# A gated mix of two attention branches: channel order of branch B's output, one ratio tile, merged write-outs, the gate turned by TensorE, and a new instruction order

## Chip, cores and metric

The kernel runs on one core of a Trainium2 chip. The metric is the device time of one execution in microseconds (us). All five engines are used: PE (TensorE, matmuls), ACT (ScalarE), DVE (VectorE), POOL (GpSimd) and SP (SyncE, which here issues nearly all DMAs). Each engine works through its own instructions strictly in order; semaphores tie them together.

## What is computed

`x` is 2048 tokens by 640 channels, 32 heads of 20 channels. Branch A is a linear attention with softmax features, branch B a segment-wise causal attention with a compressive memory; a gate per token mixes them.

```python
x = A_x
g = sigmoid((x * gate_w).sum(-1, keepdims=True))
# branch A: phi(k) = [softmax(k w_phi), softmax(-k w_phi)], same for q
o_A = (phi_q @ (phi_k^T v)) / (phi_q @ sum(phi_k) + 1e-6)
# branch B: 4 segments of 512 tokens, per head
p     = softmax(q k^T * scale + causal mask);  a_dot = p @ v
a_mem = (pq @ M) / (pq @ z + 1e-6)      # M, z: sums over earlier segments
o_B   = sigmoid(beta) * a_mem + (1 - sigmoid(beta)) * a_dot
out = g * (o_A @ A_wo) + (1 - g) * (o_B @ B_wo)
```

## The kernel before

**Order.** The program builds a graph of operations and then emits them in an order that stands in it as a table (`ORDER`, one base-36 number per operation). Two more tables say on which engine an operation with a choice runs (`CHOICE`: an evacuation of PSUM on ACT or DVE, the scaling of `E` on DVE or POOL) and which buffer each tile takes (`WHERE`). Nothing is decided at run time: each engine's queue is a fixed list, waits are derived from the data and buffer dependences.

**Stages.** Early in the span the projections of branch B for segment 0, its attention, and the keys and values of branch A (`a_k`, L887 on, and the sums over tokens `acc`, L956, and `KVZacc`) run side by side; the last `acc` addition ends at 166 us. After it come the queries of branch A, segment by segment (`a_q`: `ET` L1015, ratio round trip `zb`, `zc`, `rx`, `rr`, products L1047, matmuls L1062, `oA` L1071), beside the remaining attention of branch B, and the output matmuls (`final`, L1090/1091) per 128-token tile.

**Branch B's attention** (`b_step`, once for each of 4 segments and 8 groups of 4 heads, spread over the span up to 309 us): QK matmuls (L763), exponentials on ACT (L772), causal masks on POOL (L776), PV matmuls (L804). The PV output sits in PSUM as 4 blocks of 32 partitions, one block per head: rows 0 to 19 are the channels, row 20 the softmax denominator, already divided by 1 - sigmoid(beta) through a column of `v1B`. It is copied to `oU` (`evac`, L608 on ACT or L609 on DVE). `oU` holds two groups.

**Leaving `oU`** (end of `b_step`): per pair of groups, SP issues four DMAs that write the denominators to the DRAM tensor `dn` and four that write the channels to `opk`, one each per block of 32 partitions. With 4 segments and 4 pairs that is 64 and 64.

**The ratio** (`b_out`, once per segment): `dc` is read back from `dn` as 128 x 128 (32 KB), `rqB` is its reciprocal (L835), and L836 multiplies it by `og`, one minus the gate, which arrives in the same layout through DRAM (`gt`, one write and four reads per segment, end of `b_proj`, L476). The product is written to DRAM 20 times, once for each channel of a head (`rxB<-dc`, 4 DMAs of 160 KB), and read back as `rrB`, 128 x 5 x 512 (640 KB). `oP`, 128 x 5 x 512, holds the channels in their natural order (row p of chunk c is channel 128 c + p), so each chunk needs a ratio of its own. L844 multiplies `oP` by `rrB`, L884 adds `moT`, the memory part: for each of the 4 token tiles of a segment, matmuls L866/867, a reciprocal (L875), one DVE product from PSUM into `mo` (L876, 128 x 640) and a DMA transpose into `moT` (L473). Then `final` multiplies `oTA` and `oP` by `Wo`, whose second half is `B_wo` in the same natural order (`load_wo`).

Output tiles, `oA` and `mo` share a pool of four buffers of 1280 bytes; output tiles may take two more inside the projection weights `WB` once these are done.

Of the kernel before, what the change touches and what calls it, by code (L numbers as in the profile page):

```python
# [70 lines left out]
002211073310534000222133101014230232135210305133220
# [1108 lines left out]
```

## Time and profile before

| | us |
|---|---|
| median of 3 runs (lowest, highest) | 368.99 (367.27, 371.01) |
| the profiled execution's own time | 370.18 |
| its span, first to last instruction | 368.4 |
| busy: PE / ACT / DVE / POOL | 290.6 / 252.0 / 227.7 / 120.7 |

The mean granted TensorE clock is 0.907 of full speed. The profile's chain, followed back from the last instruction, divides the span as PE 29%, DVE 25%, DMA 22%, ACT 10%, SP's queue 9%, issue 4%. Durations and waits are those of the one profiled execution; a wait is put down to what released it last. The rows that the prediction uses stand in a section of their own below.

### The profile page before, as it was taken

The numbers are of one execution on the slowest core, as the hardware profiler recorded it, in microseconds if no ns is written. First come the engines' busy times: TensorE is split into PE (matmuls) and PEld (weight loads), VectorE is DVE, ScalarE is ACT, GpSimd is POOL, SyncE is SP. The second block draws the span as 40 slices with busy tenths as digits, with TensorE's granted clock in tenths as the row PEclk, the third lists the DMA queues.
The fourth block names the chain that finished last, engine by engine and source line by source line (L and its number), as shares of the span: only waits on it lengthen the run. The fifth ranks groups of instructions, "written<-read, shape, count | busy, mean of one in ns | idle before, by whom it ended". The sixth has DMA issues, their size and how long they took to land.

```text
span 368.4 us, 7093 instructions
## 1 busy us (share of the span) xinstructions
PE 290.6 (79%) x2811; PEld 151.1 (41%) x2852; DVE 227.7 (62%) x370; ACT 252.0 (68%) x332; POOL 120.7 (33%) x136
## 2 busy tenths in 40 slices
PE   2999899988799999699639957897997666093686
PEld 2355445544444544263324523344443323052343
DVE  1544679998999999997527832638534631443440
ACT  4377899897699999589726964888799996010011
POOL 2022653656356155642501101432434553000000
PEclk9999999999999999899868996999999955579669
DMA  7987550302424310142356996883555636735851
GB/s 216 259 168 167 93 122 1 52 2 45 74 50 69 79 33 8 14 127 75 118 145 170 155 44 153 227 158 55 121 144 158 60 85 167 182 98 128 207 146 56
DMA packets 88880, 40.80 MB, mean 111 GB/s; under 512 B 68080, under 2 KB 86416, under 8 KB 88848
## 3 DMA queue, kind: packets, MB, share of 16 engines
q1 hardware_dynamic: 88096, 39.50, 50.1%
q10 hardware_dynamic: 656, 0.82, 0.6%
q8 instruction: 22, 0.36, 0.4%
q0 software_dynamic: 96, 0.04, 0.3%
q14 instruction: 10, 0.08, 0.1%
HBM read 16.37 MB, written 13.16 MB: 80 GB/s over the span
## 4 chain that ended last, share of the span: by engine, by line
PE 29%; DVE 25%; DMA 22%; ACT 10%; SPq 9%; issue 4%; POOL 1%; DVEq 0%; ACTq 0%
PE ps L629 7%; SPq L477 7%; DVE acc L956 6%; PE ps L1090 6%; ACT expT L772 5%; DMA oTA<-oA 4%; DVE z L914 3%; DMA moT<-mo 3%; PE ps L901 3%; DMA zb<-zs 2%; PE ps L763 2%; PE ps L651 2%; DMA kT<-qkm 2%; DMA xtok<-in_A_x_dram 2%; PE ps L1091 2%
## 5 line engine op out<-in xcount | busy, mean ns | idle before, releaser
L772 ACT ACTIVATE expT<-ps 128x1024 bf16<-128x1024 f32 x128 | 124.4, 1037 | 23.2 <-PE ps L763 22.4
L776 POOL TENSOR_SCALAR_AFFINE_SELECT expT<-expT 128x512 bf16<-128x512 bf16 x96 | 69.0, 727 | 104.5 <-ACT expT L772 95.1
L629 PE MATMUL ps<-xT,WB 128*128 128x512 bf16 x192 | 50.3, 397 | 1.5 <-DVE xT L609 0.7
L608 ACT ACTIVATE out<-ps 128x640 bf16<-128x640 f32 x7 | 4.9, 704 | 52.7 <-PE ps L1091 32.6
L763 PE MATMUL ps<-qkm 20*128 20x384 bf16 (+3 forms) x320 | 22.0, 326 | 19.7 <-DVE oU L609 7.2
L772 ACT ACTIVATE ej<-ps 128x1024 bf16<-128x1024 f32 x32 | 31.6, 1046 | 6.6 <-PE ps L763 6.6
L916 POOL TENSOR_TENSOR E<-E,z 128x1280 bf16<-128x1280 bf16 x12 | 28.8, 2404 | 20.5 <-DVE z L915 17.6
L776 POOL TENSOR_SCALAR_AFFINE_SELECT ej<-ej 128x1024 bf16<-128x1024 bf16 x16 | 18.5, 1157 | 47.8 <-ACT ej L772 42.0
L1090 PE MATMUL ps<-Wo,oTA 128*128 128x512 bf16 x77 | 27.4, 439 | 7.9 <-DVE mo L876 4.8
L956 DVE TENSOR_TENSOR acc<-acc,E 64x1280 bf16<-64x1280 bf16 x31 | 31.0, 1001 | 1.7 <-POOL E L916 1.0
L1091 PE MATMUL ps<-Wo,oTA 128*128 128x128 bf16 x80 | 19.4, 242 | 11.9 <-DVE mo L876 11.5
L804 PE MATMUL ps<-expT,v1B 128*21 128x384 bf16 (+2 forms) x384 | 24.9, 331 | 4.9 <-POOL expT L776 1.6
L629 PEld LDWEIGHTS ps<-xT,WB 128*128 128x128 bf16 x200 | 18.2, 101 | 23.2 <-issue 5.7
L1090 PE MATMUL ps<-Wo,oP 128*128 128x512 bf16 x78 | 26.5, 423 | 0.0
L914 DVE TENSOR_REDUCE z<-E 128x64 f32<-128x1280 bf16 x16 | 23.7, 1479 | 3.2 <-ACT E L908 3.1
L1015 ACT ACTIVATE ET<-ps 128x512 bf16<-128x512 f32 x40 | 22.8, 614 | 3.8 <-PE ps L1010 2.3
L901 PE MATMUL ps<-WvA,xT 128*128 128x512 bf16 x77 | 22.7, 379 | 1.9 <-ACT eg L655 1.1
L908 ACT ACTIVATE E<-ps 128x640 bf16<-128x640 f32 x32 | 22.5, 708 | 1.1 <-PE ps L902 0.6
L1010 PE MATMUL ps<-xT,WqA 128*128 128x512 bf16 x91 | 21.8, 380 | 1.8 <-issue 0.8
L609 DVE CAST out<-ps 128x640 bf16<-128x640 f32 x9 | 7.4, 823 | 25.0 <-PE ps L1091 23.2
L651 PE MATMUL ps<-WvB,xT 128*128 128x512 bf16 x72 | 22.6, 393 | 0.2 <-ACT ej L772 0.2
L901 PE MATMUL ps<-WkA,xT 128*128 128x512 bf16 x73 | 21.8, 380 | 0.0
(126 smaller groups left out, 554.7 us busy)
## 6 DMA issues: line engine op xcount, KB each, us to landing
opk<-oU SPq DMA_DIRECT2D x64, 40.0 KB
oP<-opk SPq DMA_DIRECT2D x4, 640.0 KB
rxB<-dc SPq DMA_DIRECT2D x16, 160.0 KB
rx<-rc SPq DMA_DIRECT2D x16, 160.0 KB
rr<-rx SPq DMA_DIRECT2D x4, 640.0 KB
rrB<-rxB SPq DMA_DIRECT2D x4, 640.0 KB
out_dram<-out SPq DMA_DIRECT2D x16, 160.0 KB
scr<-qkm SPq DMA_DIRECT2D x16, 120.0 KB
```

The costliest lines, as they stand in the source:

```text
L477: return e.dma_start(a, b)
L629: r = e.matmul(self.pf(pt, 0, 0, LSEG), lhsT=self.WB[:, w, kc, 128 * c:128 * (c + 1)], rhs=xT[:, kc, LSEG * n:LSEG * (n + 1)], start=(kc = ...
L651: e.matmul(self.pf(pt, 0, 0, 512), lhsT=l, rhs=self.WvB[:, kc, 0:512], start=(kc == 0), stop=(kc == 4))
L763: r = e.matmul(self.pf(pts[i // 2], i % 2, c0, N), lhsT=view(32 * i, 32 * i + DH, 1, 128 * j, 128 * (j + 1)), rhs=view(32 * i, 32 * i + DH ...
L772: self.op("act", d_act(1024), lambda e, p=p, o=o: e.activation(o(), self.pbanks(pts[p], 0, 2, 512), ACT.Exp, scale=scale), W=[(pts[p], 0), ...
L776: self.op("pool", d_pool(n_el), lambda e: e.affine_select(view(), view(), pattern=pat, compare_op=ALU.is_ge, fill=0.0, base=0, channel_mul ...
L901: e.matmul(self.pf(pt, 0, 0, 512), lhsT=l, rhs=W[:, kc, 0:512], start=(kc == 0), stop=(kc == 4))
L914: self.op("dve", 1.48, lambda e: e.tensor_reduce(z[:, :], Ev(), axis=AX.X, op=ALU.add), R=[(E, 0), (E, 1)], W=[(z, "*")], claim=[rz], pr=p ...
L916: self.op(("dve", "pool"), {"pool": d_pool(1280, 2), "dve": 1.56}, lambda e: e.tensor_tensor(Ev(), Ev(), rz[:, :].rearrange("p (h o) -> p ...
L956: self.op("dve", 0.9, lambda e, src=src: e.tensor_tensor(acc[lo:lo + 64, :], acc[lo:lo + 64, :], src(), ALU.add), R=[(self.Et[t], 0), (sel ...
L1090: e.matmul(self.pf(pt, 0, 0, 512), lhsT=l, rhs=self.Wo[:, c, 0:512], start=(c == 0), stop=(c == 9))
L1091: r = e.matmul(self.pf(pt, 1, 0, 128), lhsT=l, rhs=self.Wo[:, c, 512:640], start=(c == 0), stop=(c == 9))
```

## The change

- Branch B's output rows are dealt out so that partition 4 h + r of `oP` holds channels 5 r to 5 r + 4 of head h, one per chunk. One 128 x 512 ratio then serves all five chunks: `rxB` is written once (32 KB, one DMA instead of four of 160 KB), read back as 128 KB instead of 640 KB, and L844's product reads it broadcast over the chunks. `B_wo` is loaded in that row order, and `mo` is written in it by two DVE instructions of 128 x 320 instead of one of 128 x 640.
- `opk` holds `oU` as it is, 128 rows per group with denominators and padding: one DMA of 256 KB per pair of groups instead of eight. `dc` (rows 20 of each block) and `oP` (rows 0 to 19) are both read from it.
- The gate's way through DRAM (`gt`, `og`) is gone. Four fp32 matmuls per segment (`omg` broadcast to 32 columns against an fp32 identity) put one minus the gate into PSUM in the layout of `dc`, and the product L836 reads it there. The identity costs a memset and a POOL instruction at the start.
- Output tiles may take five buffers in `WB` instead of two. Four PE spin matmuls instead of six.
- `ORDER`, `CHOICE` and `WHERE` are new throughout.

```diff
-NSPIN = 6
+NSPIN = 4
...
-CHOICE = "001100011111110001011010100001010101011111000010111011000011111111110010101001010101111001110110100000111100001101001101111111110001100101010010011011111101000001"
+CHOICE = "100111000110011010110010101110011111101111111111101101101001001111001100101000010010101111110011110100111111001101101011001100000101010001010111111010111101011001"
...
-        for i in range(2):
-            sl = Slot(self.WB.off + 10240 + 1280 * i)
+        for i in range(5):
+            sl = Slot(self.WB.off + 5120 + 1280 * i)
...
-        gt, gtT = self.gt[n % 2]
-        og = self.sbt("og", [128, 128], FP32, self.p_og)
-        self.dma("sp", gt.rearrange("q t -> t q"), self.omg[:, sl], R=[(self.omg, n)], W=[(gtT, "*")], pr=prg + 1, noncontig=True, name="gtw", issue=0.5, lat=3.0)
-        for q in range(4):
-            self.dma("sp", lambda q=q, og=og: og[q:128:4, :], gt[q:q + 1, :].rearrange("o t -> (o t)").partition_broadcast(32), R=[(gtT, "*")], W=[(og, q)],
...
-            for i in range(4):
-                self.dma("sp", dn.rearrange("(g i o) t -> i o g t", i=4, o=1)[i][:, gs, :], lambda oU=oU, i=i: oU[32 * i + DH:32 * i + DH + 1, :, :],
...
-            for i in range(4):
-                self.dma("sp", opk.rearrange("(g i d) t -> i d g t", i=4, d=DH)[i][:, gs, :], lambda oU=oU, i=i: oU[32 * i:32 * i + DH, :, :],
...
+            self.dma("sp", opk[slice(g0, g + 1, g - g0)].rearrange("g p t -> p g t"), lambda oU=oU: oU[:, :, :],
...
-        self.dma("sp", lambda: dc[:, :], dn.rearrange("h (q t) -> (h q) t", q=4), R=[(dnT, "*")], W=[(dc, "*")], pr=pr, name="dr", issue=0.4, lat=1.8)
-        self.dma("sp", lambda: oP[:, :, :], opk.rearrange("(c p) t -> p c t", p=128), R=[(opT, "*")], W=[(oP, c) for c in (0, 3)], pr=pr, name="opr", issue=0.4, lat=4.0)
+        hv = opk.rearrange("g (i r) t -> (g i) r t", r=32)
+        self.dma("sp", lambda: dc[:, :], hv[:, DH, :].rearrange("h (q t) -> q h t", q=4), R=[(opT, "*")], W=[(dc, "*")], pr=pr, name="dr", issue=0.45, lat=1.7)
+        self.dma("sp", lambda: oP[:, :, :].rearrange("p c t -> p (c t)"), hv[:, 0:DH, :].rearrange("h (d c) t -> h d (c t)", c=NCH),
...
+        gp = self.pst("og", 1)
+        def ogm(e):
+            for q in range(4):
+                b = 512 * gp.t[0]
+                r = e.matmul(self.ps[32 * q:32 * q + 32, b:b + 128], lhsT=self.omg[:, 4 * n + q:4 * n + q + 1].to_broadcast([128, H]), rhs=self.identF[:, :],
...
-        for q in range(4):
-            self.dma("sp", rx.rearrange("h f (q t) -> q h f t", q=4)[q],
-                     lambda q=q: dc[q:128:4, :].rearrange("p (o t) -> p o t", o=1).to_broadcast([32, DH, 128]),
...
+        self.dma("sp", rx.rearrange("h (q t) -> q h t", q=4), lambda: dc[:, :], R=[(dc, "*")], W=[(rxT, "*")], pr=pr, name="rxw", issue=0.5, lat=2.0)
+        self.dma("sp", lambda: rr[:, :], rx.rearrange("h (o t) -> h o t", o=1).to_broadcast([H, 4, LSEG]), R=[(rxT, "*")], W=[(rr, "*")], pr=pr, name="rxr", issue=0.45, lat=2.2)
...
-        wB = self.ins["B_wo"].rearrange("(c p) n -> p c n", p=128)
+        wB = self.ins["B_wo"].rearrange("(p c) n -> p c n", c=NCH)
```

What each engine now has: SP issues 176 DMAs instead of 320. DVE has 396 instructions instead of 372 (among them 5 more evacuations of `qkm`, 4 more of `v1B`, 2 fewer of `vA`, 2 more of `zs`, 2 more scalings of `E`, 24 products into `mo` instead of 12), ACT 326 instead of 335.

SP's queue near the end of the program, before the change, from the write-outs of the last group pairs to the read of the last ratio (`oU_319` is the last pair, `oU_300` and `oU_308` older ones, `dc_333` and `rrB_340` the last segment's ratio):

```order
L477 DMA dn<-oU_319 2x1x512 x4
L476 DMA og_322<-gt 32x128 x2
L477 DMA opk<-oU_319 20x2x512 x2
L477 DMA opk<-oU_300 20x2x512
L477 DMA dc_333<-dn 128x128
L473 DMA_TRANSPOSE moT_323<-mo_325 128x5x128
L477 DMA opk<-oU_319 20x2x512
L477 DMA opk<-oU_308 20x2x512
L477 DMA opk<-oU_319 20x2x512
L477 DMA rxB<-dc_333 640x1x128 x4
L473 DMA_TRANSPOSE moT_323<-mo_329 128x5x128
L477 DMA oP_339<-opk 128x5x512
```

The same place after it (`oU_321` is the last pair, `oU_302` the one before, `dc_330` and `rrB_341` the last ratio):

```order
L472 DMA opk<-oU_302 128x2x512
L472 DMA rr_296<-rx 128x5x512
L468 DMA_TRANSPOSE oTA_326<-oA_312 128x5x128
L472 DMA opk<-oU_321 128x2x512
L468 DMA_TRANSPOSE oTA_331<-oA_317 128x5x128
L468 DMA_TRANSPOSE moT_314<-mo_320 128x5x128
L472 DMA dc_330<-opk 128x1x128
L472 DMA oP_336<-opk 128x1x2560
L468 DMA_TRANSPOSE moT_314<-mo_316 128x5x128
L472 DMA rxB<-dc_330 4x32x128
L468 DMA_TRANSPOSE moT_314<-mo_325 128x5x128
L472 DMA rrB_341<-rxB 128x1x512
```

Between the last pair's write-out and the read of the denominators stand two transposes now; the 13 small writes of older pairs that surrounded them are gone.

SP's queue where the first ratio of branch A goes out (`zb_193` written, `zc_194` read back), before:

```order
L477 DMA dc_192<-dn 128x128
L477 DMA Wo<-in_B_wo_dram 128x5x640
L477 DMA dn<-oU_188 2x1x512
L477 DMA qks<-scr 20x3x1024
L477 DMA opk<-oU_188 20x2x512
L477 DMA dn<-oU_188 2x1x512
L477 DMA zb<-zs_193 64x512
L476 DMA gt<-omg 128x4x1
L477 DMA opk<-oU_163 20x2x512
L477 DMA zc_194<-zb 128x2x128
```

And after (`zb_192` is not numbered there; `zs_192` is its source, `zc_193` the tile read back):

```order
L472 DMA scr<-qkm_56 12x5x1024
L472 DMA Wo<-in_B_wo_dram 128x3200
L472 DMA scr<-qkm_56 12x5x1024
L472 DMA qks<-scr 20x3x1024
L472 DMA zb<-zs_192 64x512
L472 DMA zc_193<-zb 128x2x128
```

The write of `zb` still stands behind a weight load of 800 KB, with two other transfers between them; the write-outs around it have moved away.

## Rows read from the trace of the kernel before

**Rows 1.** Windows: two long stages and the tail (PE, PEld, DVE, ACT, POOL busy, clock, DMA).

```profile
37.00:166.00 129.00, 117.21 (x1180) 62.40 (x1198) 118.47 (x155) 112.56 (x146) 67.92 (x60) 0.99 0.28 55
166.00:308.60 142.60, 110.11 (x1186) 54.72 (x1199) 74.71 (x147) 112.81 (x148) 44.89 (x61) 0.88 0.62 124
308.60:368.40 59.80, 34.23 (x246) 19.12 (x248) 20.10 (x38) 5.51 (x9) 0.64 (x1) 0.74 0.55 144
```

**Rows 2.** Timeline of ACT: start, duration, and [idle before, releaser].

```profile
308.57 0.72 ACT L608 ACTIVATE oU<-ps 128x512 bf16<-128x512 f32 x1
310.86 0.60 ACT L608 ACTIVATE oU<-ps 128x512 bf16<-128x512 f32 x1 [1.57 <-PE ps L804]
...
191.13 1.94 ACT L772 ACTIVATE expT<-ps 128x1024 bf16<-128x1024 f32 x2 [6.93 <-PE ps L763]
...
223.62 1.02 ACT L772 ACTIVATE ej<-ps 128x1024 bf16<-128x1024 f32 x1 [5.79 <-PE ps L763]
```

**Rows 3.** Timeline of SP's queue in the tail: start and duration of issuing.

```profile
324.31 4.16 SPq L477 DMA_DIRECT2D dn<-oU  x7
...
331.28 0.35 SPq L477 DMA_DIRECT2D dc<-dn  x1
...
334.40 2.68 SPq L477 DMA_DIRECT2D rxB<-dc  x4
```

**Rows 4.** The chain that ended last, in order of time, in the tail.

```profile
312.42 5.93 DMA rrB<-rxB
...
331.28 1.79 DMA dc<-dn
...
340.74 6.41 DMA moT<-mo
...
348.17 1.55 DVE oP L844 x2
349.72 1.47 DVE oP L884 x2
...
351.69 0.61 PE ps L1090
...
365.40 0.70 ACT out L608
```

**Rows 5.** Timeline of DVE: two waits after 166 us.

```profile
188.84 0.95 DVE L1038 RECIPROCAL zc<-zc 128x128 f32<-128x128 f32 x1 [9.22 <-DMA zc<-zb]
...
222.07 0.82 DVE L876 TENSOR_TENSOR mo<-ps,cs 128x640 bf16<-128x640 f32 x1 [5.80 <-DMA oTA<-oA]
```

**Rows 6.** Tiles: SP's issue time per DMA, ns minimum/median/maximum.

```profile
L477 SPq DMA_DIRECT2D opk<-oU x64: 276/412/1882, 48.5 to 334.0; - x64
L477 SPq DMA_DIRECT2D dn<-oU x64: 537/584/713, 49.5 to 327.9; - x64
L477 SPq DMA_DIRECT2D rxB<-dc x16: 532/638/704, 185.4 to 336.4; - x16
L476 SPq DMA_DIRECT2D og<-gt x16: 452/523/655, 141.0 to 329.1; - x16
```

**Rows 7.** Groups by form on ACT and DVE: busy us, mean ns, idle before.

```profile
L608 ACT ACTIVATE qkm<-ps 128x512 bf16<-128x512 f32 x19 | 11.2, 598 | 8.5 <-PE ps L629 8.5
L608 ACT ACTIVATE v1B<-ps 128x640 bf16<-128x640 f32 x12 | 8.5, 711 | 0.3
L608 ACT ACTIVATE vA<-ps 128x640 bf16<-128x640 f32 x9 | 6.3, 701 | 0.2 <-PE ps L902 0.2
...
L1071 DVE SCALAR_TENSOR_TENSOR oA<-ps,g,cs 128x320 bf16<-128x320 f32 x32 | 16.0, 543 | 7.6 <-DMA moT<-mo 6.3 <-DMA oTA<-oA 1.0
...
L876 DVE TENSOR_TENSOR mo<-ps,cs 128x640 bf16<-128x640 f32 x12 | 9.7, 816 | 11.2 <-DMA oTA<-oA 5.8 <-DMA moT<-mo 4.8 <-DMA out_dram<-out 0.3
...
L1038 DVE RECIPROCAL zc<-zc 128x128 f32<-128x128 f32 x4 | 3.8, 947 | 9.2 <-DMA zc<-zb 9.2
```

**Rows 8.** The page's DMA queue: packets, MB, share of 16 engines' span.

```profile
q1 hardware_dynamic: 88096, 39.50, 50.1%
```

More of the change, by code (lines that the diff above doesn't have):

```diff
@@ L71 @@
[L71 removed]
+012345671014530143501034035310301053401354130100220132001210012313223010233001103231132200126327101642110267010435001200310260313321401321241305100262
+310403031521012313202031230103203160207210230030103413521200111214331010211321340232110023213001201030100113221103201020132033220332023023131200232304
+567010530100000530241025103410230023200332000031011260710122230021132331002041005210607114500136371000042310030812332034031302116004071514567212010130
@@ L72 @@
+000041063201340182004512303245032250031112260126270014201076021610201020601021600011230030000213003232003120300223820013030221306120101232003518021733
+0031262430013025827100153162202113070052531600371
 """
@@ L398, in memory @@
         self.p_ET.slots[1].off = et1
-        self.p_rx, self.p_mx = self.pool(1, 5120, et1), self.pool(1, 5120, et1 + 5120)
-        self.p_ry, self.p_my = self.pool(1, 5120, self.WB.off), self.pool(1, 5120, self.WB.off + 5120)
-        for p in (self.p_ry, self.p_my):
+        self.p_mx, self.p_my = self.pool(1, 5120, et1), self.pool(1, 5120, self.WB.off)
+        self.p_rx, self.p_ry = self.pool(1, 1024, et1 + 5120), self.pool(1, 1024, self.WB.off + 11520)
+        for p in (self.p_my, self.p_ry):
             p.slots[0].occ = [self.WB]
@@ L444, in memory @@
         self.zb = [dram(f"zb{i}", [2, H, LSEG], FP32) for i in range(2)]
-        self.opk = [dram(f"opk{i}", [D, LSEG], BF16) for i in range(2)]
-        self.dn = [dram(f"dn{i}", [H, LSEG], BF16) for i in range(2)]
-        self.gt = [dram(f"gt{i}", [4, 128], FP32) for i in range(2)]
-        self.rxB = [dram(f"rxB{i}", [H, DH, LSEG], BF16) for i in range(2)]
+        self.opk = [dram(f"opk{i}", [NG, 128, LSEG], BF16) for i in range(2)]
+        self.rxB = [dram(f"rxB{i}", [H, LSEG], BF16) for i in range(2)]
         self.rx = [dram(f"rx{i}", [H, DH, LSEG], BF16) for i in range(2)]
@@ L836, in b_out @@
-        self.op("dve", 0.28, lambda e: e.tensor_tensor(dc[:, :], rq[:, :], og[:, :], ALU.mult), R=[(rq, "*")] + [(og, q) for q in range(4)], W=[(dc, "*")], pr=pr, name="rqm")
-        for q in range(4):
-            self.dma("sp", rx.rearrange("h f (q t) -> q h f t", q=4)[q],
-                     lambda q=q: dc[q:128:4, :].rearrange("p (o t) -> p o t", o=1).to_broadcast([32, DH, 128]),
-                     R=[(dc, "*")], W=[(rxT, q)], pr=pr, nbytes=164e3, name="rw")
-        self.dma("sp", lambda: rr[:, :, :], rx.rearrange("h f t -> (h f) t").rearrange("(c p) t -> p c t", p=128), R=[(rxT, "*")], W=[(rr, "*")], pr=pr, nbytes=655e3, name="rr")
+        rr = self.sbt("rrB", [128, LSEG], BF16, p_r)
@@ new lines, in b_out @@
+        hv = opk.rearrange("g (i r) t -> (g i) r t", r=32)
+        self.dma("sp", lambda: dc[:, :], hv[:, DH, :].rearrange("h (q t) -> q h t", q=4), R=[(opT, "*")], W=[(dc, "*")], pr=pr, name="dr", issue=0.45, lat=1.7)
+        self.dma("sp", lambda: oP[:, :, :].rearrange("p c t -> p (c t)"), hv[:, 0:DH, :].rearrange("h (d c) t -> h d (c t)", c=NCH),
+                 R=[(opT, "*")], W=[(oP, c) for c in (0, 3)], pr=pr, name="opr", issue=0.5, lat=4.8)
+        self.op("dve", 0.95, lambda e: e.reciprocal(rq[:, :], dc[:, :]), R=[(dc, "*")], W=[(rq, "*")], pr=pr, name="rqr")
@@ new lines, in b_out @@
+        gp = self.pst("og", 1)
[3 more added lines that the diff above has]
+                r = e.matmul(self.ps[32 * q:32 * q + 32, b:b + 128], lhsT=self.omg[:, 4 * n + q:4 * n + q + 1].to_broadcast([128, H]), rhs=self.identF[:, :],
+                             start=True, stop=True, tile_position=(0, 32 * q), skip_group_check=True)
+            return r
+        self.op("pe", 0.25, ogm, R=[(self.omg, n), (self.identF, "*")], W=[(gp, 0)], claim=[dc], pr=pr, name="og")
```

91 lines of the change are left out of this document (41 added, 50 removed).

## The prediction

> **What bounds the kernel now.** Start with the windows [rows 1], which say which engine fills which stage. From 37 to 166 us DVE is busy 118.5 of 129.0 us and ACT 112.6: this stage is bound by DVE with ACT close behind. From 166 to 308.6 us ACT is busy 112.8 of 142.6 us and no engine more, so 29.8 us of it are waits. From 308.6 us to the end, 59.8 us, ACT is nearly done (5.5 us), DVE works 20.1 us and PE 34.2 us at a mean granted clock of 0.74, between the two levels of 1.2 and 2.4 GHz. This tail is latency, not work.
>
> What sets the tail is seen in two views read side by side. ACT's timeline [rows 2] ends the attention: the last `oU` is copied out at 310.86 + 0.60 = 311.46 us. Call this M; from M to the end of the span are 56.9 us. The chain [rows 4] reads the denominators only at 331.28 us, 19.8 us after M. SP's timeline [rows 3] says why: SP works off a list, with seven `dn` writes alone taking 4.16 us from 324.31 us, and the read of `dc` is behind them. So SP's queue is the bound from M to 331 us. Then follow a round trip for the ratio (four `rxB` writes, 2.68 us of issuing from 334.40 us), a transpose of `moT` that ends at 340.74 + 6.41 = 347.15 us, the products, and four output tiles from 351.69 to 365.40 us.
>
> In the stage before, the two longest waits of ACT, 6.93 us before 191.13 and 5.79 us before 223.62 us [rows 2], are for QK matmuls. DVE's timeline [rows 5] shows where they come from: DVE, in order, stands 9.22 us before `zc` (the ratio of branch A's first segment) and 5.80 us before a `mo` whose buffer an `oTA` transpose still reads, and PE waits for evacuations that stand behind these.
>
> **The change, part by part.** *SP.* By the medians [rows 6] there go 64 x 0.412 + 64 x 0.584 + 16 x 0.638 + 16 x 0.523 = 82.3 us of issuing, and the four `gt` writes; there come 16 merged writes and 4 of `rxB`, at the nearest medians 16 x 0.412 + 4 x 0.638 = 9.1 us. Where SP has slack this is worth nothing, in the tail it is on the path.
>
> *The tail, counted from M.* The new queue has the last write-out, two transposes, then `dc`. The merged write moves 256 KB. No row shows such a transfer alone; the rows on both sides are `dc` with 32 KB, 1.79 us, and `rrB` with 640 KB, 5.93 us [rows 4]. By bytes between them it takes 3.3 us, and I take that; with 0.4 us of issuing it lands at M + 3.7. The transposes are issued while it flies. `dc` takes 0.35 + 1.79 us as now: M + 5.8. From its landing at 333.07 us to the first `rxB` at 334.40 us [rows 3, 4] pass 1.3 us (reciprocal and product): M + 7.1. One `rxB` write of 32 KB, 0.64 + 1.79: M + 9.6. `rrB` of 128 KB, by bytes 2.4 us (bounds again 1.79 and 5.93), with 0.4 of issuing: M + 12.4. The last `moT` transpose stands right behind `rrB`'s issue, at M + 10.0, and takes 6.4 us as at 340.74 us: M + 16.4. The products with the ratio (1.55 us) are over before that, the additions start then. From their start to the first output matmul there are 351.69 - 349.72 = 2.0 us, to the span's end 368.4 - 349.72 = 18.7 us [rows 4]: the span would end at M + 35.1.
>
> Two things can be late instead. PE has output tiles of the segment before and `U` matmuls to do in these 16 us; four tiles took 13.7 us at mixed clock, so PE is about level, and I add 1.5 us for it, with up to 8 us as the other bound where the clock stays low. The gate's four fp32 matmuls per segment are in no row; the nearest is an output matmul of 512 columns, 0.61 us at the low clock [rows 4], so four cost between nothing (beside waits of PE) and 2.4 us; I take 0.4 us. The tail becomes 37 us instead of 56.9: **20 us gained**, with bounds of 10 (large transfers at 5.93 us, three of them slower by 2.6 to 4.1 us, PE late) and 23 (the merged write at 1.79 us).
>
> Of small pieces the profile's page shows this much: the queue's 88096 packets held 16 engines for 50.1% of 368.4 us, 33.5 ns each [rows 8]. The Trainium skill has a rule against the new form: "DMA: Bandwidth & Descriptors", section "Why a DMA increments its semaphore by 16 and not by 1", says that a DMA issued by SP is spread over the largest number of engines up to 16 that divides the slowest dimension of both sides. The new `dc` and `rxB` have a slowest dimension of 4 on the DRAM side, so by it 4 engines would carry 32 pieces of 256 bytes each instead of 8, 24 x 33.5 ns = 0.8 us more per transfer, an estimate. By that rule the two on the tail's path would cost 1.6 us and the time would come out that much longer; no row here tests it, and the sum above goes without it.
>
> *M itself.* ACT loses 5 x 0.598 + 4 x 0.711 us and gains 2 x 0.701 us of evacuations [rows 7]: 4.4 us less before M. They go to DVE. Up to the last `acc` addition the counts on DVE balance: 11 more evacuations and scalings stand against small instructions and memory updates that move behind it, so I see no gain and no loss for the first stage; a DVE that is busy 92% there has no cover for an error in this, and 5 us either way are possible. After 166 us DVE has room (74.7 of 142.6 us) for the moved evacuations and for the halves of `mo`: 24 at the duration of the nearest form, 0.543 us (`oA`, also from PSUM), are 13.0 us instead of 9.8 us. Their strided writes are in no row; at twice that price they would be 26 us, still within the room, but 4 or so of them stand on the tail's path.
>
> Of the waits, 12.7 us hang on `zc` and on the shared buffers. The `zb` write still follows the weight load, without the write-outs around it, and output tiles have three buffers more. I take half, 6.4 us, and give back 3 us because SP now stands waiting for a write-out to land before each `dc`, with transposes and `acc` moves queued behind it. So M comes 4.4 + 6.4 - 3 = **8 us earlier**, with bounds of -5 (nothing of the waits, DVE late) and +20 (ACT 29.8 us of waits largely gone).
>
> *Sum.* 368.4 - 20 - 8 = 340.4 us of span. The profiled execution's own time is 1.8 us above its span: 342.2 us. It stood 0.3% above the median, so 341 us on the runs' scale. The identity's two instructions at the start and the two spin matmuls less lie beside waits for the first loads and count nothing; if they didn't, they would be under 1 us.
>
> **Rivals.** *The waits go too.* If ACT is kept fed after 166 us, M comes 20 us earlier: 368.4 - 20 - 20 + 1.8 = 330 us. For it speaks that the waits have DMA and buffer causes; against it that the order stays a fixed list in which each round trip stalls whoever asks early. 0.15.
>
> *Only the tail, and half of it.* PE, left with seven output tiles behind the last attention, gets the low clock: the four tiles' 13.7 us and the earlier ones stretch, the tail loses 10 us and M stays: 360 us. For it: the mean clock of 0.74 now. Against: PE has more to do there without a break. 0.13.
>
> *Slower: DVE's round trips.* Branch A's ratio has four round trips, and only the first stops DVE for long now (9.22 us). In the new list all four, and the four gate products that now also wait for PE's matmuls, might. At 9.22 us each for the three other `zc` and 2.6 us (a quarter of that) each for the four products, 27.7 + 10.5 = 38 us would be added to 341: 379 us. It decides from 28 us on, where all the gain is eaten. For it: the places of `zc` on DVE are new. Against: the group of the four `zc` reciprocals has 9.2 us of idle time in all [rows 7], so the other three wait for nothing now. 0.09.
>
> *The change does little.* SP's list was long because the order was made for it; if the write-outs were never what the denominators waited for, but ACT's late copies, M to `dc` would stay and 366 us come out. Against it: at 324.31 us, 13 us after M, SP still writes `dn` [rows 3]. 0.05.
>
> **How the numbers follow.** The forecast, 341 us, own range 332 to 352, has 0.58, the rivals 0.15, 0.13, 0.09 and 0.05. A measurement of this kernel tells about 1% from no change. Range: 322 us (M 20 us earlier, tail at its bound of 23 us, less 3) to 361 us (the half tail), which leaves out the slower case, the small change and the far ends, about 0.2. Faster by over 1% (under 365.3 us): forecast, first two rivals and a little of the last, 0.87. Within 1%: 0.05. Slower: 0.08.
>
> **What would show it.** In the changed kernel's SP timeline the read of the last `dc` comes within 4 to 6 us of the last `oU` copy instead of 19.8 us; from that copy to the end are 33 to 42 us; SP has pauses in the tail. In ACT's timeline the last exponential ends near 300 us. The windows show a PE clock above 0.74 in the tail. Wrong would be: the tail still above 48 us, a `dc` read that waits over 6 us for its write-out, DVE idle over 9 us before more than one `zc` or gate product, or `mo` halves over 1 us each.

## The result

The changed kernel takes 340.63 us (median of 4 runs, 338.95 to 340.94), the kernel before 368.85 us beside it (4 runs): a ratio of 0.922, 95% interval 0.917 to 0.928. Measured again on another chip it took 339.35 us beside 373.52 us: 0.909, interval 0.905 to 0.914. The kernel before differs more between chips than the changed one, so each saving below is taken against the kernel before on the same chip. The variants ran on several chips, though: `mo_runs`, `mo_plain`, `old_order` and `eight_writes` on one (kernel before 374.74 us), `after_again`, `old_order_runs`, `runs_hq` and `four_writes` on another (373.52 us); where two savings from different chips are subtracted, one or two us are uncertain (between the two measurements above, the saving itself differs by 6 us). An execution over 1.5% above the fastest of its kernel counts as slow and is left out of the ratios.

The profiled execution took 340.44 us with a span of 338.9 us. The page divides the chain of work that ended last by engine:

```profile
PE 53%; DVE 26%; ACT 12%; DMA 7%; issue 1%; SPq 0%; ACTq 0%
```

SP's queue, 9% before, is off the chain, and DMA went from 22% to 7%. The windows by stage (first stage up to the last `acc` addition, second stage up to the last `oU` copy, tail; columns as in [rows 1]):

```profile
37.00:155.00 118.00, 116.31 (x1172) 60.93 (x1170) 108.10 (x144) 108.38 (x145) 64.77 (x53) 1.00 0.32 65
155.00:303.50 148.50, 119.42 (x1278) 59.60 (x1274) 105.18 (x181) 114.27 (x147) 47.63 (x64) 0.84 0.48 117
303.50:339.00 35.50, 27.97 (x226) 16.30 (x226) 24.98 (x36) 2.82 (x4) 0.00 (x0) 0.90 0.58 131
```

Against [rows 1] the first stage is 12 us shorter (its last `acc` addition ends at 154.3 instead of 166.2 us) and the tail, 56.9 us before, lasts 35.4 us with PE busy 79% of it. The second stage is no shorter, and DVE works 105 us in it. ACT's timeline gives M, the end of the last `oU` copy, as 302.88 + 0.60 = 303.48 us, 8.0 us earlier than in [rows 2]:

```profile
297.55 1.94 ACT L763 ACTIVATE expT<-ps 128x1024 bf16<-128x1024 f32 x2
301.94 0.60 ACT L606 ACTIVATE oU<-ps 128x512 bf16<-128x512 f32 x1 [2.45 <-PE ps L795]
302.88 0.60 ACT L606 ACTIVATE oU<-ps 128x512 bf16<-128x512 f32 x1 [0.34 <-PE ps L795]
```

SP's timeline in the tail, to be read against [rows 3] (other transposes between these left out):

```profile
303.50 0.36 SPq L472 DMA_DIRECT2D opk<-oU  x1
...
308.01 0.59 SPq L472 DMA_DIRECT2D dc<-opk  x1
...
314.50 0.56 SPq L472 DMA_DIRECT2D rxB<-dc  x1
315.10 2.13 SPq L468 DMA_TRANSPOSE moT<-mo  x1
317.67 0.55 SPq L472 DMA_DIRECT2D rrB<-rxB  x1
```

The denominators are read 4.5 us after M instead of 19.8. But from their read to the ratio's write pass 6.5 us. DVE's timeline says why:

```profile
302.19 5.85 DVE L869 TENSOR_TENSOR mo<-ps,cs 128x320 bf16<-128x320 f32 x4
...
308.48 2.99 DVE L869 TENSOR_TENSOR mo<-ps,cs 128x320 bf16<-128x320 f32 x2
...
313.20 0.94 DVE L820 RECIPROCAL rqB<-dc 128x128 f32<-128x128 bf16 x1
...
314.39 2.99 DVE L869 TENSOR_TENSOR mo<-ps,cs 128x320 bf16<-128x320 f32 x2
...
322.80 1.55 DVE L877 TENSOR_TENSOR oP<-oP,moT 128x1536 bf16<-128x1536 bf16 x2
```

Eight `mo` halves, a pitch of 1.5 us each, stand in DVE's row, and six of them ahead of the ratio's reciprocal. PE, too, waits for what follows them and then runs a whole output tile near the low clock of 1.2 GHz; in the 8 us before, it was busy 3.8 us. From 316.5 us the clock is full again, and PE is busy 19.2 us on end, up to its last output tile (first a row of PE's timeline, then the windows):

```profile
311.52 0.61 PE L1083 MATMUL ps<-Wo,oTA 128*128 128x512 bf16 x1 [3.01 <-DVE cs L864]
```

```profile
311.50:316.50 5.00, 4.97 (x20) 2.38 (x21) 4.94 (x7) 0.00 (x0) 0.00 (x0) 0.53 0.51 141
316.50:339.00 22.50, 19.16 (x170) 11.88 (x168) 12.11 (x21) 2.11 (x3) 0.00 (x0) 1.00 0.51 129
```

So the tail of the changed kernel is bound by the `mo` halves up to 311.5 us and by PE from there on. The chain that ended last has no transfer in it behind M: the ratio's round trip is ready before PE asks for it.

All 24 halves (instructions that write `mo`; ns min/median/max, first and last start):

```profile
L869 DVE TENSOR_TENSOR mo<-ps,cs x24: 1565/1787/1817, 178.3 to 315.6; 128x320 bf16<-128x320 f32 x24
```

The nearest form, `oA`, had 0.543 us [rows 7]. So the kernel came out where it was forecast with a term three times too small, and something else must have paid for it.

### The profile page after: what moved, and what is told of

Read it like the earlier page. It is cut to its first block, busy times and chain, and to the rows that moved or that the text cites. A ratio compares the mean times of both kernels' runs of the same rounds, so it can differ in the third digit from the quotient of the medians.

```text
span 338.9 us, 7011 instructions
## 1 busy us (share of the span) xinstructions
PE 293.3 (87%) x2882; PEld 152.0 (45%) x2882; DVE 255.5 (75%) x394; ACT 247.3 (73%) x323; POOL 121.5 (36%) x135
## 4 chain that ended last, share of the span: by engine, by line
PE 53%; DVE 26%; ACT 12%; DMA 7%; issue 1%; SPq 0%; ACTq 0%
PE ps L627 9%; PE ps L1083 9%; DVE mo L869 8%; ACT expT L763 7%; PE ps L894 6%; DVE acc L949 4%; PE ps L754 4%; PE ps L1055 4%; PE ps L1003 4%; PE ps L795 3%; PE ps L649 3%; DVE z L907 3%; DMA stk<-in_B_wk_dram 2%; PE ps L1084 2%; ACT ej L763 2%; DMA acc<-acc 2%
## 5 line engine op out<-in xcount | busy, mean ns | idle before, releaser
L763 ACT ACTIVATE expT<-ps 128x1024 bf16<-128x1024 f32 x128 | 123.8, 1031 | 16.4 <-PE ps L754 15.6
L767 POOL TENSOR_SCALAR_AFFINE_SELECT expT<-expT 128x512 bf16<-128x512 bf16 x96 | 71.9, 760 | 119.8 <-ACT expT L763 105.4
L869 DVE TENSOR_TENSOR mo<-ps,cs 128x320 bf16<-128x320 f32 x24 | 35.7, 1704 | 0.3
L1083 PE MATMUL ps<-Wo,oTA 128*128 128x512 bf16 x80 | 24.8, 395 | 5.1 <-DVE cs L864 3.0
L949 DVE TENSOR_TENSOR acc<-acc,E 64x1280 bf16<-64x1280 bf16 x31 | 27.7, 894 | 1.9 <-DMA acc<-acc 1.1
L1008 ACT ACTIVATE ET<-ps 128x512 bf16<-128x512 f32 x40 | 22.3, 602 | 8.1 <-PE ps L1003 7.6
L754 PE MATMUL ps<-qkm 20*128 20x128 bf16 (+3 forms) x320 | 21.1, 315 | 7.7 <-ACT expT L763 4.2
L795 PE MATMUL ps<-expT,v1B 128*21 128x384 bf16 (+2 forms) x384 | 27.2, 343 | 0.0
L909 POOL TENSOR_TENSOR E<-E,z 128x1280 bf16<-128x1280 bf16 x10 | 25.6, 2563 | 1.6 <-DVE MmI L534 0.8
L649 PE MATMUL ps<-WvB,xT 128*128 128x512 bf16 x80 | 25.2, 397 | 0.5 <-ACT eg L653 0.4
L1083 PE MATMUL ps<-Wo,oP 128*128 128x512 bf16 x80 | 24.5, 391 | 0.0
L607 DVE CAST oU<-ps 128x512 bf16<-128x512 f32 x22 | 15.0, 683 | 11.3 <-PE ps L795 11.2
```

The lines of the kernel that those rows point to most:

```text
L649: e.matmul(self.pf(pt, 0, 0, 512), lhsT=l, rhs=self.WvB[:, kc, 0:512], start=(kc == 0), stop=(kc == 4))
L754: r = e.matmul(self.pf(pts[i // 2], i % 2, c0, N), lhsT=view(32 * i, 32 * i + DH, 1, 128 * j, 128 * (j + 1)), rhs=view(32 * i, 32 * i + DH ...
L763: self.op("act", d_act(1024), lambda e, p=p, o=o: e.activation(o(), self.pbanks(pts[p], 0, 2, 512), ACT.Exp, scale=scale), W=[(pts[p], 0), ...
L767: self.op("pool", d_pool(n_el), lambda e: e.affine_select(view(), view(), pattern=pat, compare_op=ALU.is_ge, fill=0.0, base=0, channel_mul ...
L795: r = e.matmul(self.ps[32 * i:32 * i + 21, 512 * ad.t[0] + 128 * j:512 * ad.t[0] + LSEG], lhsT=vt[:, j, h, :], rhs=src[:, i, c0:c0 + N], s ...
L869: self.op("dve", d_dve(320, 1, True), lambda e, b=b, N4=N4, r=r, mo=mo: e.tensor_tensor(mo[:, :].rearrange("p (c b h d) -> p b h d c", b=2 ...
```

## Experiments

**What the `mo` writes cost.** In the change, neighbouring results of a `mo` half lie 128 bf16 values (256 bytes) apart. `mo_runs` walks the same product in another order:

```diff
-mo[...].rearrange("p (c b h d) -> p b h d c", ...)[:, b], N4()[...].rearrange("p h (d c) -> p h d c", c=NCH)
+mo[...].rearrange("p (c b h d) -> p b c h d", ...)[:, b], N4()[...].rearrange("p h (d c) -> p c h d", c=NCH)
```

> The changed kernel, with the same 24 `mo` products walked in another order (chunk outermost, then head, then the four channels), so that each writes 5 runs of 64 neighbouring bf16 values and reads PSUM in steps of 5; the values and their places are the same. Theory 1, the step from one written value to the next (256 bytes) makes the half cost 1.5 us: the half falls to 0.55 to 0.7 us, some 24 us of DVE go, the eight halves behind the last `oU` copy take 8 us less and the kernel ends at 326 to 334 us. Theory 2, the price is that of a four-dimensional walk or of PSUM read in pieces: the half stays at 1.3 us or more and the time within 338 to 343 us. Theory 3, the half gets cheap but the exponentials and the last output products set the time anyway: 0.55 to 0.7 us and 337 to 341 us.

`mo_plain` writes `mo[:, 320 * b:320 * b + 320]` straight on:

> The changed kernel, with the 24 `mo` products written in the natural order of the channels, as the kernel before did, but still as two halves; the memory part of branch B is so added to other channels than in the reference. Theory 1: 0.54 us for a half, as the oA halves take, and a time within 2 us of that of the kernel that writes runs of 64. Theory 2: only here does the half fall to 0.54 us, and the kernel ends at 326 to 334 us. Theory 3: 0.54 us and 337 to 341 us.

`runs4` has the walk `p b h c d`:

> The changed kernel with the `mo` products walked head by head and chunk by chunk, the four channels of a chunk innermost: runs of 4 neighbouring bf16 values (8 bytes), the next run 256 bytes on. It asks how long a run must be. If the price is one of every jump, a quarter of the 1.0 to 1.3 us that single values cost over runs of 64: 0.75 to 0.8 us for a half. If only the innermost step counts: 0.48 us, as with runs of 64. If the four-dimensional walk costs: over 1 us.

Measured: `mo_runs` 323.3 us, ratio 0.862 (0.859 to 0.866); `mo_plain` 322.85 us, 0.861 (0.857 to 0.864); `runs4` 320.6 us in a single execution. The instructions that write `mo`, of `mo_runs` and of `runs4`:

```profile
L869 DVE TENSOR_TENSOR mo<-ps,cs x24: 475/480/493, 177.9 to 295.9; 128x320 bf16<-128x320 f32 x24
```

```profile
L869 DVE TENSOR_TENSOR mo<-ps,cs x24: 474/480/492, 178.3 to 295.5; 128x320 bf16<-128x320 f32 x24
```

Theory 1 holds, with 3 us more than it promised: only the step between values written one after the other costs, 1.3 us for a half. Runs of 8 bytes are as good as a straight write, although a jump follows every fourth value, and PSUM read in steps of five values costs nothing. With this gone M is 288.0 us and the tail 31.5 us. The chain of `mo_runs` behind M:

```profile
287.98 3.87 DMA opk<-oU
291.87 2.37 DMA dc<-opk
294.26 0.96 DVE rqB L820
295.25 0.29 DVE dc L830
295.56 3.83 DMA rxB<-dc
299.41 2.63 DMA rrB<-rxB
302.06 1.02 DVE oP L835 x2
...
305.24 0.38 PE ps L1083
```

Here the tail is the round trip that the prediction drew, and after it four output tiles without a pause. `mo_runs` is faster than both kernels, with the same values written to the same places.

**Parts against order.** `old_order` has all parts of the change in the kernel before's three tables (the merged operations at the place of the last of theirs); `old_order_runs` adds the walk of `mo_runs`. `after_again` is the changed kernel.

```diff
-ORDER, CHOICE, WHERE of the changed kernel
+ORDER, CHOICE, WHERE of the kernel before, its numbers carried over to the new operations
```

> The parts of the change (one 128x512 ratio, one write per pair, gate by TensorE, `mo` in halves, permuted output weights) in the order, engine choice and buffer choice of the kernel before: the one write of a pair stands where the last of the eight stood, the ratio's write where the last of four stood, the gate matmul just ahead of the product that reads it. Theory 1, the end behind the last `oU` copy is shortened by the parts and not by the order: that stretch lasts 36 to 44 us, the first stage ends near 166 us as before, and the kernel takes 344 to 356 us. Rival, most comes from the new order: the stretch stays over 48 us and the kernel takes 360 us or more. Second rival, the order does nothing: within 3 us of the changed kernel's 340.6 us.

> The parts of the change in the order of the kernel before, with the `mo` halves written in runs of 64 (0.48 us each). It asks what the parts are worth without the strided writes and without the new order. Theory 1, the parts shorten the end (56.9 us in the kernel before, 45.2 with the strided writes) and the new order shortens the first stage and the end's queue: the stretch behind the last `oU` copy is 38 to 42 us, the last `acc` addition still ends at 165 to 168 us, and the ratio to the kernel before is 0.93 to 0.95. Rival, in the old order the strided writes were hidden behind the exponentials: 0.955 to 0.97, as with them. Second rival, the parts do it all: 0.87 or less, as in the new order.

> The changed kernel itself, beside the kernels of this group on one chip. Expected: the ratio of the first measurement, 0.917 to 0.928, with `mo` halves of 1.5 to 1.8 us.

| | order | `mo` | median us | less than before, same chip | last `acc` ends | M | M to end |
|---|---|---|---|---|---|---|---|
| before | old | one, 0.82 us | 368.85 | | 166.2 | 311.5 | 56.9 |
| `old_order` | old | single values | 362.04 | 12.7 | 167.2 | 315.9 | 45.2 |
| `old_order_runs` | old | runs | 344.59 | 28.9 | 166.4 | 303.0 | 42.5 |
| `after_again` | new | single values | 339.35 | 34.2 | 154.1 | 302.3 | 35.5 |
| `mo_runs` | new | runs | 323.30 | 51.4 | 153.9 | 288.0 | 31.5 |

The three effects add up nearly alike whichever stands first: the parts take 29 us off, the strided writes put 16 to 17 us on (28.9 - 12.7, 51.4 - 34.2), the new tables take 22 us off (34.2 - 12.7, 51.4 - 28.9); each of these four differences is between savings from two chips. `after_again` missed its own range of 0.917 to 0.928 (0.909), with halves as slow as before. `old_order`, 0.966 (0.962 to 0.969), missed theory 1, 344 to 356 us, by just those writes. Without them, in `old_order_runs`, the 42.5 us of tail lie half a microsecond over what was expected, and the ratio, 0.924 (0.919 to 0.929), a little under. SP's timeline of `old_order_runs` shows what the parts need from the order:

```profile
303.84 2.83 SPq L479 DMA_DIRECT2D opk<-oU  x4
311.16 0.57 SPq L479 DMA_DIRECT2D dc<-opk  x1
```

Four merged writes still queue up around M = 303.0 us, and the denominators are read 8.2 us after M, against 3.9 in `mo_runs`. In this order DVE also stands 13.9 us in all before three of the four gate products, for PE's matmuls; in the changed kernel it stands 0.1 us.

**One write for a pair.** `eight_writes` is the changed kernel with

```diff
-e.dma_start(opk[two groups], oU[:, :, :])
+for lo, hi in 4 x (one denominator row) + 4 x (twenty rows): e.dma_start(opk[two groups][lo:hi], oU[lo:hi, :, :])
```

> The changed kernel in its own order, with each pair's write-out issued as eight DMAs again (four of one denominator row, four of twenty rows, each for two groups) in place of one. Theory 1, SP's time for a pair, 4.2 us against 0.4 to 0.6, was part of what the tail and the end of the second stage waited for: the denominators are read 3 to 4 us later behind the last `oU` copy, and the kernel takes 343 to 350 us. Rival, in the new order SP stands off the path (PE and DVE end last there): 340 to 342 us.

It took 352.5 us, ratio 0.942 (0.939 to 0.945): 22.3 us less than the kernel before on its chip, where the changed kernel has 34.2 less. That is 12 us for the eight writes, more than expected (13 by the medians; the two kernels ran on different chips). The chain of its page, where the changed kernel has 0% for SP's queue, and its SP timeline:

```profile
PE 52%; DVE 21%; ACT 8%; SPq 8%; DMA 8%; issue 3%
```

```profile
316.05 4.00 SPq L809 DMA_DIRECT2D opk<-oU  x8
322.81 0.59 SPq L473 DMA_DIRECT2D dc<-opk  x1
```

Theory 1 has the sign, but neither the size nor the place: M comes at 313.9 us, 10.4 us later than in the changed kernel, and the tail is 36.4 us, only 1.0 longer, although the denominators are read 4.4 us later behind M. Its first stage ends at 153.5 us, as in the changed kernel. So the 4 us for a pair hurt in the second stage, where loads and transposes stand in the same queue.

**Four writes of the ratio.** `four_writes` is `mo_runs` with the ratio written by four DMAs, twenty times each, 640 KB for a segment:

```diff
-dma_start(rx.rearrange("h (q t) -> q h t", q=4), dc[:, :])
+for q in range(4): dma_start(rx.rearrange("h f (q t) -> q h f t", q=4)[q], dc[32 * q:32 * q + 32, :] repeated 20 times)
```

> The kernel with runs of 64, and the ratio's write as the kernel before had it: four DMAs for a segment, each of which repeats 32 rows twenty times (640 KB for a segment in all); the read stays 128 KB. Theory 1, issues and landing of the ratio stand on the chain of the end: from the issue of the ratio's write to that of its read 5.5 to 7 us in place of 3.85, the kernel 2 to 5 us slower than with one write (ratio 0.868 to 0.876). Rival, SP and the DMA engines have room there: 0.860 to 0.866.

333.1 us, ratio 0.891 (0.887 to 0.896): some 10 to 12 us more than `mo_runs` (10.9 by the savings, 11.7 against `runs_hq` below on the same chip), twice the most expected. SP's timeline for the first and for the last segment, then a row of the waits between 155 and 290 us (total, times, longest):

```profile
180.12 3.37 SPq L834 DMA_DIRECT2D rxB<-dc  x4
...
304.58 3.89 SPq L834 DMA_DIRECT2D rxB<-dc  x4
311.12 0.56 SPq L473 DMA_DIRECT2D rrB<-rxB  x1
```

```profile
DVE oP L840 <- DMA rrB<-rxB: 11.2, 2, 6.4
```

From the first issue of the ratio's writes to that of its read are 6.5 us instead of 3.85, as expected, but M too comes at 296.1 instead of 288.0 us: DVE waits 11.2 us for `rrB` in the second stage, where `mo_runs` waits 3.4. Whether the four issues or the twentyfold bytes cost more was not taken apart.

**The form of the 32 KB transfers.** `runs_hq` is `mo_runs` with

```diff
-dc[:, :], hv[:, DH, :].rearrange("h (q t) -> q h t", q=4)
+dc[:, :], hv[:, DH, :].rearrange("h (q t) -> h q t", q=4)
...
-rx.rearrange("h (q t) -> q h t", q=4), dc[:, :]
+rx.rearrange("h (q t) -> (h q) t", q=4), dc[:, :]
```

and the gate by one bf16 matmul.

> The kernel with runs of 64, and the denominators laid on the partitions as head by quarter in place of quarter by head: read and written with 32 or 128 outermost pieces in place of 4, the ratio's write one contiguous 32 KB. The gate is one bf16 matmul of 128 columns in place of four fp32 ones of 32 rows; VectorE writes its bf16 operand beside the gate (one small instruction more for a segment). Theory 1, the four-piece form costs landing time: the write lands 1 to 2 us earlier than the 3.83 us of the kernel with runs, the read 0 to 1 us earlier than 2.37, both on the chain of the end, and the kernel is 1 to 3 us faster (ratio 0.853 to 0.860). Rival, the landing of 32 KB is a fixed cost: 3.5 to 3.9 us again and a ratio of 0.860 to 0.864. If the pieces of 128 cost more than they save: the write over 4 us, the ratio 0.864 or more.

321.4 us, ratio 0.861 (0.857 to 0.865). Against `mo_runs` no difference that the intervals tell apart. Its chain:

```profile
290.82 2.13 DMA dc<-opk
294.27 4.27 DMA rxB<-dc
```

The read is 0.24 us shorter, the write 0.44 us longer. Theory 1 does not hold, since the write does not land earlier. The ratio is in the rival's range, but the write's 4.27 us lie above its 3.5 to 3.9 us (one execution of each kernel). These 32 KB cost 2.1 to 2.4 and 3.8 to 4.3 us, and neither form is shown to be better.

**The first stage.** `old_choice` is `mo_runs` with one table of the kernel before.

```diff
-CHOICE of the changed kernel
+CHOICE of the kernel before
```

> The kernel with runs of 64, in the new order and with the new buffers, but with the engine of every operation that may run on two engines taken from the kernel before (71 of 162 change: mostly copies out of PSUM between ACT and VectorE, and eight of the sixteen normalisations of branch A between VectorE and GpSimd, 10 of which VectorE does by either list in all but others). It asks whether the first stage, whose last `acc` addition ends at 154 us in the new order and at 166 in the old one, is shorter by its order or by its engines. Theory A, the order: 152 to 157 us and a ratio of 0.860 to 0.885. Theory B, the engines: 162 us or later and a ratio over 0.885, near the 0.924 of the old order with runs.

(Of the sixteen normalisations one runs on VectorE and seven on GpSimd by both lists; eight change sides.) Three of its executions took 349.5, 350.4 and 353.8 us, ratio 0.939 (0.931 to 0.946), slower than the old order with its own engines (0.924). In its profiled execution, the longest of its four (356.9 us), the last `acc` addition ends at 176.3 us, so that place is an upper figure; DVE is busy 111.7 and ACT 108.8 of the 139.0 us from 37 to 176 us. The numbers are in theory B's range, but they lie beyond the old order too, so the engines alone do not explain the 12 us: the new order gains nothing here with the old engines. The new engines in the old order were not run.

One mechanism can be seen by itself. In the kernel before, DVE's and GpSimd's timelines have at one place

```profile
143.80 2.95 DVE L956 TENSOR_TENSOR acc<-acc,E 64x1280 bf16<-64x1280 bf16 x1
```

```profile
143.70 2.36 POOL L916 TENSOR_TENSOR E<-E,z 128x1280 bf16<-128x1280 bf16 x1
```

though an `acc` addition has a median of 0.82 us. The longest in the changed kernel is 1.14 us. `apart` is the kernel before with three such instructions moved behind the next reduction (each line is a place in `ORDER`):

```diff
-pk product, z reduction
+z reduction, pk product
...
-v1B cast, z reduction
+z reduction, v1B cast
...
-acc addition, z reduction
+z reduction, acc addition
```

> The kernel before, with three instructions of VectorE's first stage each moved behind the reduction of branch A that follows it in VectorE's row: one bf16 product `pk`, the second cast of the gate's ones into `v1B`, and one `acc` addition. In the kernel before each of the three began while GpSimd ran a `tensor_tensor` of 2.36 to 2.92 us (`E` by `z`) and lasted 2.5 to 2.95 us, where the same form elsewhere takes 0.81, 0.47 and 0.82 us. Theory, the instruction stands still until GpSimd's ends, and such pairs are part of what the first stage lost in the old order: the longest `acc` addition falls from 2.95 to 1.3 us or less, the two casts to 0.5 us each, the stage ends 3 to 5 us earlier than 166 us and the kernel takes 1 to 5 us less (ratio 0.987 to 0.997). Rival, the three were late for another reason: they keep 2 to 3 us in their new places, and the stage ends at 166 us as before.

369.39 us against 371.25, ratio 0.994 (0.990 to 0.998); the stage ends at 162.9 us, 3.3 us earlier. DVE's and GpSimd's timelines of `apart`:

```profile
105.27 2.98 DVE L963 TENSOR_TENSOR acc<-acc,E 64x1280 bf16<-64x1280 bf16 x1
...
143.27 1.55 DVE L963 TENSOR_TENSOR acc<-acc,E 64x1280 bf16<-64x1280 bf16 x1
```

```profile
105.22 2.35 POOL L923 TENSOR_TENSOR E<-E,z 128x1280 bf16<-128x1280 bf16 x1
...
141.78 2.36 POOL L923 TENSOR_TENSOR E<-E,z 128x1280 bf16<-128x1280 bf16 x1
```

The moved `pk` product fell from 2.52 to 1.14 us, the cast from 2.60 to under 0.5, the moved addition from 2.95 to 1.55: it missed the expected 1.3, since it still begins 0.87 us before GpSimd's product ends. Another addition, 0.88 us before, slid beside a GpSimd product and now takes 2.98 us. Each product that began in this way, in either kernel, ended 0.7 us after GpSimd's. In the kernel before that addition had begun 0.19 us ahead of GpSimd's product, and there GpSimd's lasted 2.92 instead of 2.36 us. So the theory holds in both directions. Over the first stage these stretches add 7.2 us to DVE's instructions in the kernel before, 4.5 in `apart` and 0.4 in the changed kernel, so they can be some 7 of the 12 us; the stage of `apart` ended 3.3 us earlier, in one execution of each kernel. The rest of the gain was not taken apart.

## Why the prediction was right, and where it was not

- *The time and the tail.* 341 us came out as 340.6, the 37 us from M to the end as 35.4. But the path that the sum M + 35.1 follows, the ratio's round trip, is the one that ended last in `mo_runs` and not in the changed kernel: ratio written at M + 7.6 (said 7.1), read at M + 11.4 (9.6), additions at M + 15.6 (16.4), from there to the end 16.0 us (18.7), 31.5 in all. Even there the additions came near their time by another way: they followed the products with the ratio and waited for no `moT` transpose, and the last transpose, issued at 300.00 us, had landed within 3.5 us, not 6.4. In the changed kernel the three steps are M + 11.0, 14.2 and 19.3, because of the `mo` halves, and PE, which the prediction called about level, was busy without a wait from 311.5 us on. That the tail came to 35.4 us is luck: `mo` halves and PE's work fill the time that was forecast for transfers.
- *SP as the bound from M to 331 us.* The chain of the kernel before shows this only from 319.97 us on. The first 8.5 us behind M belong to the ratio of the segment before, its write, the read of 5.93 us [rows 4] and its products:

```profile
308.54 3.86 DMA rxB<-dc
...
318.38 1.56 DVE oP L844 x2
319.97 1.25 SPq L473
```

- *Transfers.* With issue, in `mo_runs`, the merged write took 3.87 us (3.7 said), the read of `dc` 2.37 (2.14), `rrB` 2.63 (2.8). The ratio's write was mis-sized: 3.83 us instead of 2.43.
- *The rule of the Trainium skill* ("DMA: Bandwidth & Descriptors", section "Why a DMA increments its semaphore by 16 and not by 1") was not borne out as a price here: by the estimate drawn from it the forms of `runs_hq` should have saved 0.8 us on each transfer, and they landed 0.24 us earlier and 0.44 us later. No run shows on how many engines either form ran.
- *M, 8 us earlier.* For the parts alone the number comes out, 311.5 to 303.0 in `old_order_runs`, 8.5 us, but not all of its terms: the waits of ACT for QK matmuls between 155 and 303 us fell from 19.4 to 13.3 us (half of the waits, 6.4 us, was said), while the 4.4 us of evacuations taken off ACT are a matter of `CHOICE` and not in that kernel. For the kernel as changed it was right by cancellation: the new tables brought M 15.0 us (303.0 to 288.0), 12.5 of them in the first stage, and the strided writes took 15.5 us back.
- *Steps that failed.* "Where SP has slack this is worth nothing": the term was put at nothing ahead of M, but each of the two parts, put back alone, moves M, eight writes for a pair by 10.4 us, four writes of the ratio by 8.1. "No gain and no loss for the first stage": it gained 12 us. It was counted in instructions, and the count left out that the same DVE instruction takes 0.8 or 3 us by what GpSimd runs beside it (about 7 us of DVE's time; the rest is open). "24 at the duration of the nearest form, 0.543 us": they took 1.79, and the outer bound, twice the price, was too low as well; with them DVE was busy 35.7 us instead of the 10.5 of `mo_runs`, and these 25 us cost 16 to 17. The sign of wrongness that the prediction named, halves over 1 us, did appear.
- *Rivals.* Long stops of DVE before all four ratios did not come: before `zc` it waits 2.7 us in all (9.2 before), before the reciprocals of `dc` not at all. That rival's sum has a slip (a quarter of 9.22 us is 2.3 and not 2.6, so 37 us would be added and not 38). The low clock returned for one tile only (window above), not for the tail. "The waits go too", M 20 us earlier and 330 us, is what happens once the strided writes are gone, 23.5 us and 323, but 12.3 of the 23.5 come ahead of the last `acc` addition, where that rival did not look.

## What to carry to other kernels

Before you deal out data in a new order, ask how far apart two successive results of an instruction land; let the innermost loop write neighbours, even only four of them, and take the steps on the reading side. A new layout is best measured in the old order of instructions too: only there is its worth seen apart from that of the order. A forecast that comes true is to be checked term by term, since here two errors of 12 to 15 us hid each other.

## What the hardware showed that was not expected

- A VectorE product that wrote single bf16 values 256 bytes apart took 1.57 to 1.82 us for 128x320, one that wrote runs of 4, 64 or 320 took 0.48 us. The Trainium skill, "SBUF — State Buffer", section "Door 1: The DMA port swizzle (why `[64,N]` ≈ `[32,N]`)", says that SBUF has lines of 16 bytes and that an access which moves to a new line each time pays a penalty; the trace agrees, with 1.3 us as its price for this form, and shows that runs of four values (8 bytes) avoid it; that the lines are the cause here is not shown apart from that.
- A bf16 product of two SBUF tiles on VectorE that begins beside a GpSimd product stands until that one ends: 2.95 instead of 0.82 us. Reductions beside such a product keep their 1.47 to 1.49 us. The same page's section "Who interferes with whom" says that a VectorE instruction with two SBUF inputs contends with a GpSimd instruction that reads SBUF, that the ports which the two share are an exclusive lock, and that on trn2 reductions never contend; the trace agrees on all three, with the figures above.
- The same kernel before took medians of 368.9 to 374.7 us on the chips of these groups, the changed one 339.4 and 340.6: a ratio taken on one chip did not hold to a per cent on the next.
